# PV in groups of four heads, and a fifth late bank per block, with the quartic of three of the five on GpSimd

## Chip, cores and metric

One core of a Trainium2 chip. The metric is the device time of one execution, in us (median of the runs).

## The reference

One transformer block of 2048 tokens, width 448, on a layer-normalized input: attention with 16 heads of 28, and a gated two-layer GELU network of width 1792.

```python
xn = _layernorm(A_x)
scores = jnp.einsum("bhqd,bhkd->bhqk", q, k) * Dh ** -0.5     # 16 heads, 2048 x 2048
o = jnp.einsum("bhqk,bhkd->bhqd", _softmax(scores), v)
s = o.transpose(...).reshape(B, S, D) @ wo
g = _silu(_gelu(xn @ w1 + b1) @ w2 + b2)
return x + s * g
```

## The kernel before

The attention is 16 blocks (4 groups of 4 heads, by 4 chunks of 512 queries). A block has 64 banks: 16 key tiles of 128 keys for each of 4 heads, each bank 128 keys by 512 queries of scores in PSUM. Bank m belongs to head m % 4. The banks go round in a ring of six. They are handled in units of three (`UB`), two in block 0: TensorE writes a unit of scores, ScalarE turns it into P with one exponential, and TensorE multiplies P with V (PV) into one accumulator, with head j in column group 32 j.

Four banks of each of the blocks 1 to 14 are *late*: ScalarE leaves them out, and VectorE works out the exponential as a quartic polynomial, in six passes.

```python
# late bank: evacuation, then p_exp2 (all on VectorE)
tensor_scalar(ysb, ring, c0, c1, mult, add)                   # L991, frees the PSUM bank
tensor_scalar(v, ylo, EXP_SC / 65536.0, None, mult)           # L1004
scalar_tensor_tensor(u, v, EXP_A, v, add, mult)               # L1005
scalar_tensor_tensor(u, u, EXP_B, u, add, mult)               # L1007
scalar_tensor_tensor(u, v, EXP_D, u, mult, add)               # L1009
scalar_tensor_tensor(plate, ysb, 2.0 ** -9, u, mult, add)     # L1011, bf16 bits of the exponential
# then one PV matmul of its own for this bank, when it is ready (L1019)
...
# p_exps: ScalarE, one unit                                     L969
eng.activation(K.P[:, p0:p0 + n, :], K.ring[:, b0:b0 + n, :], ACTF.Exp, scale=SM_SCALE)
...
# p_pv: one group of PV matmuls for each unit, so 3 heads at a time, or 2 (L1052)
```

The order of each engine's program is fixed when the kernel is built. A list scheduler runs through all tasks with an assumed duration for each, and emits next the task that it believes can start first (among tasks of that engine within 0.1 us of it, the one of highest priority). On the chip each engine then works through its program in that order and waits on semaphores. So an assumed duration does not change what is computed, but it decides where in an engine's program a task stands.

## Time and profile before

| | before |
|---|---|
| time, us | 507.67 |
| profiled span, us | 505.4 |
| ScalarE busy, us | 478.8 |
| TensorE / VectorE / GpSimd busy, us | 452.5 / 379.0 / 74.2 |
| waits of ScalarE for scores, us | 7.4 |
| granted TensorE clock (share of full speed) | 0.965 |

ScalarE is busy for 95% of the span and hardly waits, so its work sets the time. TensorE also looks full, but it waits for ScalarE.

### The profile page before, as it was taken

The page shows a single profiled execution, that of the slowest core. Times are in us where ns is not written, and L with a number is a line of the kernel's source. Part 1 is how long each engine was busy: PE and PEld are TensorE (multiplying, and loading weights), DVE is VectorE, ACT ScalarE, POOL GpSimd, SP SyncE. Part 2 cuts the span into 40 slices and gives each one's busy share as a digit, 9 for nine tenths or more (in the row PEclk, how much of TensorE's full clock was granted, in tenths as well). Part 3 has the DMA queues.
Part 4 walks back from the last instruction along what each step waited for, and adds up shares of the span by engine and source line. Part 5 has one row for each costly group of instructions (what it writes and reads, how often), then busy time and mean ns, then how long its engine had stood idle before and what let it go on. Part 6 is the DMA issues. An engine that isn't in the chain of part 4 may idle for free.

```text
span 505.4 us, 8696 instructions
## 1 busy us (share of the span) xinstructions
PE 452.5 (90%) x3507; PEld 146.0 (29%) x3507; DVE 379.0 (75%) x640; ACT 478.8 (95%) x385; POOL 74.2 (15%) x93
## 2 busy tenths in 40 slices
PE   6899899998999999999999999766999999999884
PEld 2433223332222222222222222212333233332442
DVE  6823997879688898988888888832576868588545
ACT  3899999999999999999999999997899999999993
POOL 5661311031011111011101010211001001010100
PEclk9999999999699999999999999956999999999989
DMA  8801000000000000000000000000001010101211
GB/s 249 258 11 23 1 1 1 0 1 1 2 1 0 1 0 1 2 2 0 1 1 0 1 3 0 1 0 0 1 2 36 2 36 2 38 0 38 75 40 36
DMA packets 8503, 10.98 MB, mean 22 GB/s; under 512 B 2448, under 2 KB 6992, under 8 KB 8464
## 3 DMA queue, kind: packets, MB, share of 16 engines
q1 hardware_dynamic: 8464, 10.44, 6.8%
q8 instruction: 27, 0.44, 0.4%
q14 instruction: 12, 0.10, 0.1%
HBM read 8.61 MB, written 1.84 MB: 21 GB/s over the span
## 4 chain that ended last, share of the span: by engine, by line
PE 39%; ACT 38%; issue 15%; DVE 7%; ACTq 0%; DVEq 0%
ACT P L969 38%; PE ring L942 9%; PE misc L890 9%; PE acc L1052 7%; PE misc L627 3%; PE misc L847 3%; PE acc L714 1%; PE acc L1019 1%; DVE qT L793 1%; DVE qT L783 1%; PE ring L627 1%; DVE w L1087 1%; DVE x_sb L1009 1%; DVE x_sb L991 1%; PE ring L807 1%
## 5 line engine op out<-in xcount | busy, mean ns | idle before, releaser
L969 ACT ACTIVATE P<-ring 128x1536 bf16<-128x1536 f32 (+1 forms) x352 | 438.0, 1473 | 7.7 <-PE ring L942 7.4
L942 PE MATMUL ring<-qT,kT 32*128 32x512 bf16 (+1 forms) x1216 | 139.1, 355 | 25.6 <-ACT P L969 20.9
L1052 PE MATMUL acc<-P,vaug 128*32 128x512 bf16 (+1 forms) x1160 | 130.9, 355 | 0.0
L942 PEld LDWEIGHTS ring<-qT,kT 32*128 32x128 bf16 x1216 | 37.1, 92 | 148.4 <-ACT P L969 127.7
L847 PE MATMUL misc<-xnT,w 128*128 128x512 bf16 x224 | 63.5, 388 | 0.4 <-DVE qT L793 0.2
L890 PE MATMUL misc<-w,h 128*128 128x448 bf16 x224 | 54.6, 363 | 2.7 <-DVE qT L783 0.9
L1052 PEld LDWEIGHTS acc<-P,vaug 128*32 128x32 bf16 x1160 | 33.2, 94 | 64.7 <-issue 60.7
L991 DVE TENSOR_SCALAR x_sb<-ring 128x512 int32<-128x512 f32 x56 | 38.6, 689 | 17.4 <-PE ring L942 16.3
L860 DVE TENSOR_SCALAR h<-misc,b1c 128x512 bf16<-128x512 f32 x56 | 41.8, 747 | 11.8 <-PE misc L847 11.4
L1113 POOL CAST rhi<-rc 128x512 bf16<-128x512 f32 x15 | 13.4, 891 | 245.0 <-DVE rc L1109 169.8
L1005 DVE SCALAR_TENSOR_TENSOR x_sb<-x_sb 128x512 f32<-128x512 f32 x56 | 41.8, 746 | 1.0
L1011 DVE SCALAR_TENSOR_TENSOR x_sb<-x_sb 128x512 uint16<-128x512 int32 x56 | 41.1, 734 | 1.0
L1009 DVE SCALAR_TENSOR_TENSOR x_sb<-x_sb 128x512 f32<-128x512 f32 x56 | 40.9, 730 | 0.9
L1007 DVE SCALAR_TENSOR_TENSOR x_sb<-x_sb 128x512 f32<-128x512 f32 x56 | 40.7, 727 | 1.1
L788 POOL TENSOR_TENSOR qsq<-qT 128x512 bf16<-128x512 bf16 x15 | 18.6, 1243 | 141.8 <-DVE qT L783 110.6
L890 PEld LDWEIGHTS misc<-w,h 128*128 128x128 bf16 x224 | 17.2, 99 | 28.9 <-issue 14.7
L895 DVE TENSOR_TENSOR w<-misc,b2b 128x448 bf16<-128x448 f32 x16 | 10.0, 622 | 19.7 <-PE misc L890 19.5
L1004 DVE TENSOR_SCALAR x_sb<-x_sb 128x512 f32<-128x512 uint16 x56 | 24.4, 436 | 0.2
L872 ACT ACTIVATE h<-h 128x7168 bf16<-128x7168 bf16 x4 | 24.4, 6164 | 0.0
L847 PEld LDWEIGHTS misc<-xnT,w 128*128 128x128 bf16 x224 | 15.5, 98 | 29.4 <-issue 11.2
L1019 PE MATMUL acc<-x_sb,vaug 128*32 128x512 bf16 x56 | 21.9, 392 | 0.2 <-DVE x_sb L1011 0.2
L627 PE MATMUL misc<-xnT,wq 128*128 128x512 bf16 x56 | 17.6, 435 | 2.7 <-DVE qT L793 1.7
(127 smaller groups left out, 336.4 us busy)
## 6 DMA issues: line engine op xcount, KB each, us to landing
x_sb<-in_A_x_dram SPq DMA_DIRECT2D x4, 448.0 KB, 6.4
h<-in_A_x_dram SPq DMA_DIRECT2D x4, 448.0 KB, 3.3
w<-in_B_w_dram SPq DMA_DIRECT2D x1, 1568.0 KB, 12.8
w<-in_B_w_dram SPq DMA_DIRECT2D x1, 1344.0 KB, 7.3
out_dram<-h SPq DMA_DIRECT2D x6, 224.0 KB, 1.9
h<-in_A_wqkv_dram SPq DMA_DIRECT2D x1, 672.0 KB, 4.8
out_dram<-h SPq DMA_DIRECT2D x4, 112.0 KB, 1.7
wo<-in_A_wo_dram SPq DMA_DIRECT2D x16, 24.5 KB
```

The costliest lines, as they stand in the source:

```text
L627: ins = eng.matmul(bank, w[:, kt, g * 128:(g + 1) * 128], K.xnT[:, kt, c * 512:(c + 1) * 512], start=(kt == 0), stop=(kt == KT - 1))
L847: ins = eng.matmul(bank, K.w1[:, kt, ft * 128:(ft + 1) * 128], K.xnT[:, kt, c * 512:(c + 1) * 512], start=(kt == 0), stop=(kt == KT - 1))
L860: yield _Task(DVE, lambda eng: eng.tensor_scalar(dst, bank, K.b1c[:, ft:ft + 1], None, op0=ALU.add), [tok, K.b_b1c], wr, 0.75, 0.0, 2)
L890: ins = eng.matmul(ps, hv[:, ft, t * 128:(t + 1) * 128], K.w2[:, ft, :], start=(ft == 0), stop=(ft == FT - 1))
L942: return eng.matmul(K.ring[:, RB[m], col:col + nq], K.kT[32 * j:32 * j + 32, g, t * 128:(t + 1) * 128], K.qT[32 * j:32 * j + 32, g, c * 51 ...
L969: return eng.activation(K.P[:, p0:p0 + n, :], K.ring[:, b0:b0 + n, :], ACTF.Exp, scale=SM_SCALE)
L991: yield _Task(DVE, lambda eng, m=m, i=i: eng.tensor_scalar(K.ysb[i], K.ring[:, RB[m], :], SM_SCALE * LOG2E * 65536.0, 127.0 * 65536.0, op0 ...
L1005: yield _Task(DVE, lambda eng: eng.scalar_tensor_tensor(u, v, EXP_A, v, op0=ALU.add, op1=ALU.mult), [tv], [tu], 0.75, 0.0, 4)
L1007: yield _Task(DVE, lambda eng: eng.scalar_tensor_tensor(u, u, EXP_B, u, op0=ALU.add, op1=ALU.mult), [tu], [tu], 0.75, 0.0, 4)
L1009: yield _Task(DVE, lambda eng: eng.scalar_tensor_tensor(u, v, EXP_D, u, op0=ALU.mult, op1=ALU.add), [tv, tu], [tu], 0.75, 0.0, 4)
L1011: yield _Task(DVE, lambda eng: eng.scalar_tensor_tensor(K.plate[k].bitcast(dt.uint16), y, 2.0 ** -9, u, op0=ALU.mult, op1=ALU.add), [ty, t ...
L1052: return eng.matmul(K.acc[32 * j:32 * j + 32, q0:q0 + nq], K.vaug[:, t, 4 * g + j, :], K.P[:, PB[m], col:col + nq], tile_position=(0, 32 * ...
```

## The change

The intent is to take more exponentials from ScalarE. A fifth late bank per block is not expected to fit on VectorE, so in blocks 4 to 14 GpSimd takes the middle of three of the five; VectorE keeps their first and last pass. PV runs over four heads at a time, and a late bank fills the place in a group that another late bank of the same head has left free.

```diff
-    for _r in (5, 17, 29, 41): ...
-        LATE.add(_m)
+    if _b < C:
+        LATE.update(range(_m, 64 * _b + 46, 12))       # four, on VectorE
+    else:
+        LATE.update((_m + 6, _m + 30))                 # two on VectorE
+        GP.update((_m, _m + 18, _m + 36))              # three with GpSimd
...
+    def p_gexp2(self, m, i):
+        def ts(o, a, s0, s1, op0, op1, rd, wr):        # GpSimd, planned with 0.72 us
+        def tt(o, a, b, op, rd, wr):                   # GpSimd, planned with 1.1 us
+        yield ts(v, lo, EXP_SC / 65536.0, 0.5 * EXP_A, ALU.mult, ALU.add, [ty], [tv])
+        yield tt(z, v, v, ALU.mult, [tv], [tz])
+        yield ts(z, z, EXP_C, None, ALU.add, ALU.bypass, [tz], [tz])
+        yield tt(z, z, v, ALU.mult, [tv, tz], [tz])
+        yield ts(z, z, EXP_D, None, ALU.add, ALU.bypass, [tz], [tz])
+        yield tt(z, z, v, ALU.mult, [tv, tz], [tz])
+        yield ts(z, z, EXP_E, None, ALU.add, ALU.bypass, [tz], [tz])
+        # last pass on VectorE: plate = y * 2^-9 + z
...
-        for u in range(NU):                            # PV by units of three
+        for q in range(MTOT // 4):                     # PV by four heads, late banks in the holes,
+            ms = list(range(4 * q, 4 * q + 4))         # or as a fifth matmul of the group
```

The new buffers `v` and `z` (512 fp32 each) lie in the keys of group 0, which nothing reads from block 4 on.

More of the change, by code (lines that the diff above doesn't have):

```diff
@@ L29 @@
 MTOT = NBLK * T * 4
-LATE = set()
+LATE, GP = set(), set()
 for _b in range(1, NBLK - 1):
-    for _r in (5, 17, 29, 41):
-        _m = 64 * _b + _r
-        while (_m - 64) % UB != UB - 1:
-            _m += 1
-        LATE.add(_m)
-UNITS, RB, PB, RPREV, PPREV = [], {}, {}, {}, {}
+    _m = 64 * _b + 4
+    while (_m - 64) % UB != UB - 1:
+        _m += 1
+    if _b < C:
[3 more added lines that the diff above has]
+        GP.update((_m, _m + 18, _m + 36))
+LATE |= GP
+UNITS, RB, PB, RPREV, PPREV, UOF = [], {}, {}, {}, {}, {}
 _last, _plast, _p = {}, {}, 0
@@ L48 @@
     for _k, m in enumerate(_ms):
+        UOF[m] = len(UNITS) - 1
         RB[m] = _b0 + _k
@@ L60 @@
 EXP_SC, EXP_A, EXP_B, EXP_D = 1.1449707906804418, 2.2275165815584925, 18.59640770523752, -75.73931899211772
+EXP_C = EXP_B - 0.5 * EXP_A * EXP_A
+EXP_E = -0.25 * EXP_A * EXP_A * (EXP_B - 0.25 * EXP_A * EXP_A) - 0.5 * EXP_A * EXP_D
 LN_EPS = 1e-5
@@ L322, in alloc @@
         self.plate = [xf[:, 5120 + 512 * i:5632 + 512 * i] for i in range(4)]
+        self.pv_, self.pz = (self.kT[:, 0, 1024 * i:1024 * (i + 1)].bitcast(f32) for i in range(2))
         self.x2 = self.h[:, :, 3584:5376].rearrange("p c (t d) -> p c t d", d=D)
         self.b_y, self.b_pl = [B() for _ in range(3)], [B() for _ in range(4)]
-        self.b_ev, self.b_eu = B(), B()
+        self.b_ev, self.b_eu, self.b_pv, self.b_pz = B(), B(), B(), B()
         self.b_xn = [[B() for _ in range(4)] for _ in range(3)]
@@ L363, in schedule @@
         K.exp_u = -1
+        K.exp_m = -1
+        K.late_ready = []
+        K.gfree = True
         K.sc_u = -1
@@ L974, in p_exps @@
             K.exp_u = u
+            K.exp_m = UNITS[u][0][-1]
             if u >= NU - 2:
@@ L994, in p_late @@
                 K.ring_rel[m] = True
-                K.spawn(K.p_exp2(m, i), m)
+                K.spawn(K.p_gexp2(m, i) if m in GP else K.p_exp2(m, i), m)
+    def p_gexp2(self, m, i):
+        K = self
+        yield ("until", lambda: len(K.pls) > 0 and K.gfree)
+        K.gfree = False
+        k = K.pls.pop(0)
+        v, z, y, lo = K.pv_, K.pz, K.ysb[i], K.ylo[i]
+        tv, tz, ty = K.b_pv, K.b_pz, K.b_y[i]
+        if tv.w is None:
+            for c in range(C):
+                tv.r += K.b_kT[0][c].r
+                tz.r += K.b_kT[0][c].r
+        def ts(o, a, s0, s1, op0, op1, rd, wr):
+            return _Task(POOL, lambda eng: eng.tensor_scalar(o, a, s0, s1, op0=op0, op1=op1), rd, wr, 0.72, 0.0, 4)
+        def tt(o, a, b, op, rd, wr):
+            return _Task(POOL, lambda eng: eng.tensor_tensor(o, a, b, op), rd, wr, 1.1, 0.0, 4)
+        yield ts(v, lo, EXP_SC / 65536.0, 0.5 * EXP_A, ALU.mult, ALU.add, [ty], [tv])
[5 more added lines that the diff above has]
+        yield ts(z, z, EXP_E, None, ALU.add, ALU.bypass, [tz], [tz])
+        yield _Task(DVE, lambda eng: eng.scalar_tensor_tensor(K.plate[k].bitcast(dt.uint16), y, 2.0 ** -9, z,
+                                                              op0=ALU.mult, op1=ALU.add),
+                    [ty, tz], [K.b_pl[k]], 0.75, 0.0, 3)
+        K.ys.append(i)
+        K.gfree = True
+        K.late_ready.append((m, k))
     def p_exp2(self, m, i):
@@ L1015, in p_exp2 @@
         K.ys.append(i)
-        b, j, pc, end, s = K.pieces(m)
-        g, t = b // C, pc[0][0]
-        yield ("until", lambda: K.pv_done[64 * b + 3] and K.ready([K.b_pl[k]], 0.1))
-        yield _Task(PE, lambda eng: eng.matmul(K.acc[32 * j:32 * j + 32, :], K.vaug[:, t, 4 * g + j, :], K.plate[k],
-                                               tile_position=(0, 32 * j), start=False, stop=False, skip_group_check=True),
-                    [K.b_pl[k], K.b_v[0 if g == 0 else 1][t]], [K.b_acc], 0.25, 0.1, 1.2)
-        K.pls.append(k)
-        K.late_left[b] -= 1
+        K.late_ready.append((m, k))
     def p_pv(self):
@@ L1030, in p_pv @@
         K.pv_started = True
-        for u in range(NU):
-            ms = UNITS[u][1]
-            parts, cur = [], []
-            for m in ms:
-                cur.append(m)
-                if K.pieces(m)[3]:
-                    parts.append(cur)
-                    cur = []
-            parts.append(cur)
-            for part in parts:
-                if not part:
-                    continue
-                first = K.sub_of(part[0])
-                yield ("until", lambda: K.exp_u >= u and K.E_done >= first - 1 and (
-                    not K.pieces(part[-1])[3] or K.late_left[part[-1] // 64] == 0))
-                fl, rd = [], []
-                for m in part:
-                    b, j, pc, end, s = K.pieces(m)
-                    g = b // C
-                    for t, q0, nq, col in pc:
-                        def f(eng, m=m, t=t, j=j, g=g, q0=q0, nq=nq, col=col):
-                            return eng.matmul(K.acc[32 * j:32 * j + 32, q0:q0 + nq], K.vaug[:, t, 4 * g + j, :],
-                                              K.P[:, PB[m], col:col + nq],
-                                              tile_position=(0, 32 * j), start=(t == 0), stop=(t == T - 1),
-                                              skip_group_check=True)
-                        fl.append(f)
-                        rd += [K.b_P[PB[m]], K.b_v[0 if g == 0 else 1][t]]
-                def fall(eng, fl=fl):
-                    ins = None
-                    for f in fl:
-                        ins = f(eng)
-                    return ins
-                yield _Task(PE, fall, rd, [K.b_acc], 0.18 + 0.05 * len(part) + 0.02 * (len(fl) - len(part)), 0.1,
-                            lambda: 1.2 if K.exp_u - K.pv_u > 4 else 6)
-                for m in part:
-                    K.pv_done[m] = True
-                if end:
-                    K.spawn(K.p_epi(b) if b < NBLK - 1 else K.p_epi4(s), 0.5)
-            K.pv_u = u
@@ new lines, in p_pv, with f, fall @@
+        for q in range(MTOT // 4):
+            ms = list(range(4 * q, 4 * q + 4))
+            first, end = K.sub_of(ms[0]), K.pieces(ms[-1])[3]
+            b = q // 16
+            yield ("until", lambda: K.exp_m >= ms[-1] and K.E_done >= first - 1 and (
+                not end or len([x for x in K.late_ready if x[0] // 64 == b]) == K.late_left[b]))
+            late = []
+            for m, k in list(K.late_ready):
+                hole = (4 * q + m % 4) in LATE and all(m % 4 != x[0] % 4 for x in late)
+                if m // 64 == b and (end or len(K.late_ready) - len(late) > 2 or (
+                        hole and K.ready([K.b_pl[k]]))):
+                    late.append((m, k))
+            for x in late:
+                K.late_ready.remove(x)
+            K.late_left[b] -= len(late)
+            src = [(m, K.P[:, PB[m], :], K.b_P[PB[m]]) for m in ms if m not in LATE]
+            src += [(m, K.plate[k], K.b_pl[k]) for m, k in late]
+            src = sorted(src[:4], key=lambda x: x[0] % 4) + src[4:]
+            fl, rd = [], []
+            for kk in range(4):
+                for m, ap, tok in src:
+                    _, j, pc, _, s = K.pieces(m)
+                    g = b // C
+                    if kk >= len(pc):
+                        continue
+                    t, q0, nq, col = pc[kk]
+                    def f(eng, t=t, j=j, g=g, q0=q0, nq=nq, col=col, ap=ap):
+                        return eng.matmul(K.acc[32 * j:32 * j + 32, q0:q0 + nq], K.vaug[:, t, 4 * g + j, :],
+                                          ap[:, col:col + nq], tile_position=(0, 32 * j), start=(t == 0),
+                                          stop=(t == T - 1), skip_group_check=True)
+                    fl.append(f)
+                    rd += [tok, K.b_v[0 if g == 0 else 1][t]]
+            def fall(eng, fl=fl):
+                ins = None
+                for f in fl:
+                    ins = f(eng)
+                return ins
+            yield _Task(PE, fall, rd, [K.b_acc], 0.36 if len(fl) < 5 else 0.6, 0.1,
+                        lambda: 1.2 if K.exp_u - K.pv_u > 4 else 6)
+            for m in ms:
+                K.pv_done[m] = True
+            K.pls += [k for _, k in late]
+            K.pv_u = UOF[ms[-1]]
+            if end:
+                K.spawn(K.p_epi(b) if b < NBLK - 1 else K.p_epi4(first - NBLK + 1), 0.5)
```

## The prediction

> **What bounds the kernel now.** I read the page's busy shares first, then the groups split by shape, then who waited for whom, then the timeline of ScalarE, and last the timelines of GpSimd and VectorE. The busy line of the page:
>
> ```profile
> PE 452.5 (90%) x3507; PEld 146.0 (29%) x3507; DVE 379.0 (75%) x640; ACT 478.8 (95%) x385; POOL 74.2 (15%) x93
> ```
>
> Two engines look full, TensorE (90%) and ScalarE (95%). The groups and ScalarE's own waits tell which one sets the time:
>
> ```profile
> L969 ACT ACTIVATE P<-ring 128x1536 bf16<-128x1536 f32 x264 | 368.4, 1590 | 7.3 <-PE ring L942 7.0
> L969 ACT ACTIVATE P<-ring 128x1024 bf16<-128x1024 f32 x88 | 96.1, 1123 | 0.4 <-PE ring L942 0.3
> ...
> PEld ring L942 <- ACT P L969: 127.7, 282, 1.1
> ...
> ACT P L969 <- PE ring L942: 7.4, 7, 4.8
> ```
>
> 352 exponentials wait for TensorE 7 times, 7.4 us in all, 4.8 us of it once. TensorE's score matmuls wait 282 times for ScalarE to release a bank, 0.45 us each on average (127.7 / 282). So ScalarE is the bound and TensorE runs ahead of it. ScalarE's timeline shows the same in long unbroken stretches:
>
> ```profile
> 49.24 83.48 ACT L969 ACTIVATE P<-ring 128x1536 bf16<-128x1536 f32 x66 [0.49 <-PE ring L942]
> 133.82 187.40 ACT L969 ACTIVATE P<-ring 128x1536 bf16<-128x1536 f32 x148 [1.10 <-PE ring L942]
> 321.23 1.28 ACT L872 ACT_TABLE_LOAD   x1
> 322.53 24.38 ACT L872 ACTIVATE h<-h 128x7168 bf16<-128x7168 bf16 x4
> 346.92 1.28 ACT L874 ACT_TABLE_LOAD   x1
> 348.21 2.37 ACT L969 ACTIVATE P<-ring 128x1536 bf16<-128x1536 f32 x2
> 355.33 17.83 ACT L969 ACTIVATE P<-ring 128x1536 bf16<-128x1536 f32 x14 [4.75 <-PE ring L942]
> ```
>
> The records overlap, so their mean (1590 ns) is not the pitch. Starts seen one by one in the timeline give it: 199.31, 200.65, 201.98 (three-bank units, 1.33 us apart), 202.88 (0.90 us after a two-bank one). One bank is 1.33 - 0.90 = 0.43 us of ScalarE. The other holes are a start of some 15 us with few exponentials, the 1.1 us at 133 (granted clock 0.67 there), the 4.75 us after the GELU (clock 0.5 until about 350), and a tail of some 9 us after the last exponential.
>
> **What the Trainium skill says.** Three places bear on it.
> "SBUF — State Buffer", section "Who interferes with whom": a VectorE instruction with two SBUF inputs and a GpSimd instruction that reads SBUF exclude each other for a whole instruction; the one that comes second waits. The trace agrees:
>
> ```profile
> 203.10 1.15 POOL L788 TENSOR_TENSOR qsq<-qT 128x512 bf16<-128x512 bf16 x1 [10.16 <-DVE qT L783]
> ...
> 203.39 1.41 DVE L1005 SCALAR_TENSOR_TENSOR x_sb<-x_sb 128x512 f32<-128x512 f32 x1
> ```
>
> L1005 usually takes 0.69 us (median of its 56); begun 0.29 us after the GpSimd product it takes 1.41, that is it waits until about 204.1 and then runs its 0.69. A VectorE evacuation from PSUM beside the same kind of product kept its usual 0.74 us.
> "GPSIMD Engine Reference", section "Engine selection": two-input elementwise work is about twice as slow there as on VectorE, one-input work about as fast. In the trace the two-input forms take 1.04 us at best against 0.69 (1.5 times), and a one-input, two-operation tensor_scalar of 448 columns 0.718.
> "TensorE: Matmul & The Clock Gate", Part 3: small matmuls in different column groups run at the same time, so a fourth tile is nearly free. Here a PV group of three heads shows 0.40 us, five or six matmuls 0.61, eight 0.82: about 0.21 us for each pass, whatever it holds.
>
> **The change part by part.**
> *Late banks.* Before: four per block in blocks 1 to 14, 56. After: four in blocks 1 to 3 and five in 4 to 14, 12 + 55 = 67. ScalarE loses 11 banks: 11 x 0.43 = 4.7 us. Of a block of ScalarE time, 17.33 x 1.33 + 4 x 0.90 = 26.7 us, 26.3 remain. This is on the path and is the one gain I count in full.
> *VectorE.* A late bank now costs L991, L1004, L1005, L1007, L1009, L1011: 0.69 + 0.44 + 0.75 + 0.73 + 0.73 + 0.73 = 4.07 us, 56 times, 228 us. After, 34 of this kind (138 us) and 33 that keep only the first and last pass, 1.42 us each (47 us): 185 us, 43 less. VectorE is not the bound, so this buys slack only, and part of it goes back into waits for the shared port.
> *GpSimd.* 33 chains of four tensor_scalar and three products. Estimated tensor_scalar at 512 columns, from the 448-column row and the 0.23 us of the 1-column ones: 0.23 + 512 x (0.718 - 0.23) / 448 = 0.79. A product is 1.05 at its fastest, and each dependent step adds about 0.08 (the gap between the cast L1113 and the difference L1114). Chain: 4 x 0.79 + 3 x 1.05 + 7 x 0.08 = 6.9 us. Per block three chains, 20.6 us, and the work it has already, 0.61 + 1.05 for the normalization and about half a square of q, 2.3 us: 23 of 26.3 us without contention. VectorE's two-input passes after the change hold the shared port for about (2 x 3 + 5) x 0.69 = 7.6 us of a block, 29%. If a GpSimd step meets one with that chance and waits half of it, that is 0.1 us a step, 2.1 us a block. So 25 of 26.3 us: tight, but it should fit. A chain with its two VectorE passes is then some 7.6 + 1.4 = 9 us.
> *PV.* Passes before: about one for each of the 352 units and one for each of the 56 late banks, some 410. After: 256 groups of four heads, in whose holes most late banks fit, and perhaps 30 additional passes. 120 passes of 0.21 us, about 25 us of TensorE, all beside ScalarE work: it takes away some of the 90% and lets TensorE wait longer for banks. On the path only in the 7.4 us that ScalarE waits; I count nothing.
> *Cost of lateness.* The order of each engine's instructions is fixed beforehand with assumed durations: in the diff 0.72 for a GpSimd tensor_scalar and 1.1 for a product, so 6.2 us and some 0.5 for steps. The real chain is by my estimate 0.2 to 1 us longer, and queues add to it by the third chain of a block. The last pass on VectorE, the PV group that takes the bank and the normalization's matmuls stand in fixed places and would wait. TensorE has about 0.45 us of slack per unit, so only a lag beyond that reaches ScalarE. If one chain in ten costs 0.45 us that is 1.5 us for 33; with queues in the normalization counted too I put it at 1.5 us in all, a choice and not a measurement.
>
> Sum: 507.8 - 4.7 + 1.5 = 504.6, say **504.5 us**.
>
> **The rivals.**
> *GpSimd becomes the bound.* For: 25 of 26.3 us is already 95%, and the shared port is claimed by both engines; the records of L1114 have a median of 1.37 us against a minimum of 1.05, and the cast L1113 0.94 against 0.61, so waiting is usual even now. If every step waits as those do (0.33 us), a chain is 6.9 + 7 x 0.33 = 9.2 us and a block needs 27.6 + 2.3 = 30 us, 3.6 more than ScalarE: some 40 us in 11 blocks, 540 us. Against: these waits come while VectorE does 16 us of late passes per block; after the change it does 8 + 4. A middle case, 1 us per block over, gives 514.
> *The waits move into the fixed order.* GpSimd keeps up on average, but each late chain holds VectorE (last pass) or TensorE (PV, normalization) for 1 to 2 us. VectorE then evacuates projections late, TensorE waits for a bank and ScalarE for scores. With 0.3 us for each of 33 chains, 10 us: 513. Against: today's collisions of 0.7 us on VectorE leave ScalarE unbroken for 187 us.
> *The hole after the GELU closes.* TensorE, freed of PV passes, may have scores ready there: up to 4.75 us more gain, 500. Against: that hole comes from a long chain of projections and the 14 matmuls of one output tile at half clock, put before the scores; PV has no part in it. It can as well grow by a few us with the new order.
> *PV in four makes TensorE the gain.* If TensorE were the true bound, 25 us would come off, 480. The 282 waits of TensorE for ScalarE speak against it.
>
> **Range and chances.** The best case is 4.7 us and most of the GELU hole, about 500; the usual one 503 to 506; the two bad rivals 510 to 515, which I give one chance in six together. Range 500.5 to 511. Faster by over 2% needs under 497.7, which the 4.7 us cannot give even with the whole of the hole and nothing lost elsewhere: 3%. Slower by over 2% is over 518, GpSimd well over its block: 7%. Within: 90%.
>
> **What would show it right or wrong.** Right: 253 three-bank units where there were 264 and 99 of two banks, pitches still 1.33 and 0.90; ScalarE's waits for scores still below 10 us; GpSimd busy some 230 to 270 us more, in blocks 4 to 14, with chains of about 7 us and idle time at the end of each block; VectorE's busy time down by 30 to 40 us; fewer PV passes and TensorE waiting longer for ScalarE. Wrong: ScalarE's waits at some 15 us or more, with VectorE waiting for GpSimd before its last pass or TensorE for late banks; GpSimd without idle time between chains; GpSimd products well over 1.4 us.

## More of the kernel before

The experiments ran in three rounds, each on another chip and each with the kernel before beside them (e1 to e4: 507.86 us, e5 to e8: 508.11, e9 to e12: 508.14). In the round of the changed kernel the kernel before takes 507.67 us (four runs, 507.16 to 508.96).

## The result

The changed kernel takes 595.26 us (four runs, 594.31 to 597.43). The ratio is 1.173 (95% interval 1.169 to 1.177). Here and below, a ratio is the mean time of one kernel's fast runs over that of the other's of the same rounds, so it is not quite the ratio of the medians quoted. The result is correct.

The busy line of the page, after the change:

```profile
PE 463.8 (78%) x3507; PEld 147.2 (25%) x3507; DVE 371.9 (63%) x574; ACT 482.9 (82%) x385; POOL 386.0 (65%) x324
```

ScalarE fell from 95% to 82%, GpSimd rose from 15% to 65%. GpSimd's 65% is an average over a span in which the chains run only from 134 us on, and pause from 382 to 416 us, at the GELU (369 to 394) and after it. From the waits after the change (engine and line, what it waited for, us in all, times, longest):

```profile
ACT P L980 <- PE ring L953: 90.8, 61, 7.8
DVE x_sb L1033 <- POOL kT L1022: 77.8, 32, 4.3
...
PEld misc L858 <- DVE h L871: 30.2, 27, 3.8
```

This is a chain of waits. VectorE stands before its last pass (L1033) until GpSimd has finished, 32 times of 33 and 2.4 us each. Meanwhile it does not evacuate projections (L871), TensorE waits for their bank (30.2 us, 5.1 before), the scores behind them come late, and ScalarE waits 90.8 us where it had waited 7.4. The chain of work that ended last, of the page, names the source:

```profile
POOL 54%; PE 18%; ACT 11%; issue 9%; DVE 8%; POOLq 0%; ACTq 0%; DVEq 0%
POOL kT L1022 30%; POOL kT L1025 21%; ACT P L980 10%; PE misc L901 4%; PE ring L953 3%; PE acc L1095 3%; POOL rlo L1157 2%; DVE x_sb L1033 2%; PE misc L638 1%; POOL rhi L1156 1%; PE acc L725 1%; DVE x_sb L1003 1%; PE misc L858 1%; PE misc L1181 1%; DVE h L871 1%
```

GpSimd is not in that line of the profile of before (TensorE 39%, ScalarE 38%, issue 15%, VectorE 7%). One chain, from GpSimd's timeline (start, duration, line, operation):

```profile
157.37 0.94 POOL L1022 TENSOR_SCALAR kT<-x_sb 128x512 f32<-128x512 uint16 x1
158.40 1.35 POOL L1025 TENSOR_TENSOR kT<-kT 128x512 f32<-128x512 f32 x1
159.84 1.81 POOL L1022 TENSOR_SCALAR kT<-kT 128x512 f32<-128x512 f32 x1
161.73 1.26 POOL L1025 TENSOR_TENSOR kT<-kT 128x512 f32<-128x512 f32 x1
163.08 1.49 POOL L1022 TENSOR_SCALAR kT<-kT 128x512 f32<-128x512 f32 x1
164.65 1.26 POOL L1025 TENSOR_TENSOR kT<-kT 128x512 f32<-128x512 f32 x1
166.00 1.49 POOL L1022 TENSOR_SCALAR kT<-kT 128x512 f32<-128x512 f32 x1
```

It takes 10.1 us (157.37 to 167.49). The three additions of a constant take 1.49 to 1.81 us each. The first step, an operation of the same name with *two* arithmetic operations, took 0.62 us when nothing disturbed it. Chains start 11.7 us apart on average (134.21 to 227.88, eight intervals), with other GpSimd work between them. Three of them are 35 us, and a block of ScalarE has 26.3. That is 8.8 us too much in each of 11 blocks, 97 us as a rough estimate.

### The profile page after: what moved, and what is told of

The parts are those of the page before. It is cut to its first block, busy times and chain, and to the rows that moved or that the text cites. A ratio compares the mean times of both kernels' runs of the same rounds, so it can differ in the third digit from the quotient of the medians.

```text
span 592.5 us, 8929 instructions
## 1 busy us (share of the span) xinstructions
PE 463.8 (78%) x3507; PEld 147.2 (25%) x3507; DVE 371.9 (63%) x574; ACT 482.9 (82%) x385; POOL 386.0 (65%) x324
## 4 chain that ended last, share of the span: by engine, by line
POOL 54%; PE 18%; ACT 11%; issue 9%; DVE 8%; POOLq 0%; ACTq 0%; DVEq 0%
POOL kT L1022 30%; POOL kT L1025 21%; ACT P L980 10%; PE misc L901 4%; PE ring L953 3%; PE acc L1095 3%; POOL rlo L1157 2%; DVE x_sb L1033 2%; PE misc L638 1%; POOL rhi L1156 1%; PE acc L725 1%; DVE x_sb L1003 1%; PE misc L858 1%; PE misc L1181 1%; DVE h L871 1%
## 5 line engine op out<-in xcount | busy, mean ns | idle before, releaser
L980 ACT ACTIVATE P<-ring 128x1536 bf16<-128x1536 f32 (+1 forms) x352 | 441.5, 1364 | 92.4 <-PE ring L953 90.8
L953 PE MATMUL ring<-qT,kT 32*128 32x512 bf16 (+1 forms) x1216 | 150.6, 385 | 31.5 <-ACT P L980 25.3
L1022 POOL TENSOR_SCALAR kT<-kT 128x512 f32<-128x512 f32 x99 | 155.9, 1574 | 8.3
L1025 POOL TENSOR_TENSOR kT<-kT 128x512 f32<-128x512 f32 x99 | 130.3, 1316 | 7.7
L1095 PE MATMUL acc<-P,vaug 128*32 128x512 bf16 (+1 forms) x1149 | 107.4, 388 | 3.2 <-DVE x_sb L1033 2.5
L858 PE MATMUL misc<-xnT,w 128*128 128x512 bf16 x224 | 73.1, 443 | 28.7 <-DVE h L871 20.7
L1022 POOL TENSOR_SCALAR kT<-x_sb 128x512 f32<-128x512 uint16 x33 | 30.9, 938 | 66.9 <-DVE x_sb L1003 44.8
L1033 DVE SCALAR_TENSOR_TENSOR x_sb<-x_sb,kT 128x512 uint16<-128x512 int32 x33 | 25.2, 765 | 77.8 <-POOL kT L1022 77.8
L871 DVE TENSOR_SCALAR h<-misc,b1c 128x512 bf16<-128x512 f32 x56 | 41.8, 746 | 30.2 <-PE misc L858 30.1
L1003 DVE TENSOR_SCALAR x_sb<-ring 128x512 int32<-128x512 f32 x67 | 45.9, 685 | 22.1 <-PE ring L953 22.0
L858 PEld LDWEIGHTS misc<-xnT,w 128*128 128x128 bf16 x224 | 17.2, 104 | 64.0 <-DVE h L871 30.2
L1054 DVE SCALAR_TENSOR_TENSOR x_sb<-x_sb 128x512 uint16<-128x512 int32 x34 | 32.2, 948 | 0.6
L1050 DVE SCALAR_TENSOR_TENSOR x_sb<-x_sb 128x512 f32<-128x512 f32 x34 | 30.6, 899 | 0.5
L1052 DVE SCALAR_TENSOR_TENSOR x_sb<-x_sb 128x512 f32<-128x512 f32 x34 | 30.1, 886 | 0.4
L1048 DVE SCALAR_TENSOR_TENSOR x_sb<-x_sb 128x512 f32<-128x512 f32 x34 | 29.2, 859 | 0.4
```

Of the source, the lines that this page charges most:

```text
L858: ins = eng.matmul(bank, K.w1[:, kt, ft * 128:(ft + 1) * 128], K.xnT[:, kt, c * 512:(c + 1) * 512], start=(kt == 0), stop=(kt == KT - 1))
L871: yield _Task(DVE, lambda eng: eng.tensor_scalar(dst, bank, K.b1c[:, ft:ft + 1], None, op0=ALU.add), [tok, K.b_b1c], wr, 0.75, 0.0, 2)
L953: return eng.matmul(K.ring[:, RB[m], col:col + nq], K.kT[32 * j:32 * j + 32, g, t * 128:(t + 1) * 128], K.qT[32 * j:32 * j + 32, g, c * 51 ...
L980: return eng.activation(K.P[:, p0:p0 + n, :], K.ring[:, b0:b0 + n, :], ACTF.Exp, scale=SM_SCALE)
L1003: yield _Task(DVE, lambda eng, m=m, i=i: eng.tensor_scalar(K.ysb[i], K.ring[:, RB[m], :], SM_SCALE * LOG2E * 65536.0, 127.0 * 65536.0, op0 ...
L1022: return _Task(POOL, lambda eng: eng.tensor_scalar(o, a, s0, s1, op0=op0, op1=op1), rd, wr, 0.72, 0.0, 4)
```

## The experiments

Theories: **F**, the one-operation form of the addition (second operation bypass) is slow in itself. **T**, additions with fp32 in and out, in place, are slow, whatever the form. **B**, GpSimd's throughput is the bound. **O**, the fixed order was planned with durations that are too short, and engines stand waiting at fixed places. **P**, GpSimd and VectorE lock each other out of a shared port. **V**, the new PV order is the loss.

| run | edit | us | ratio to before, 95% |
|---|---|---|---|
| changed kernel | | 595.26 | 1.173 (1.169 to 1.177) |
| e1_twoop | additions as two operations | 527.93 | 1.040 (1.037 to 1.042) |
| e2_pv4_only | PV in four, late banks as before | 506.49 | 0.998 (0.996 to 1.001) |
| e3_five_dve | five late banks, all on VectorE | 535.84 | 1.056 (1.053 to 1.059) |
| e4_one_gp | one chain per block in place of three | 563.59 | 1.109 (1.106 to 1.112) |
| e5_dur | changed kernel, planned with measured durations | 563.80 | 1.109 (1.105 to 1.112) |
| e6_twoop_dur | e1, planned with measured durations | 521.95 | 1.027 (1.025 to 1.030) |
| e7_one_gp_dur | e4, planned with measured durations | 532.34 | 1.047 (1.044 to 1.050) |
| e8_six | six steps in place of seven | 515.23 | 1.017 (1.012 to 1.023) |
| e9_memset | e8 with memsets for GpSimd's steps | 501.75 | 0.989 (0.987 to 0.991) |
| e10_two_gp | two six-step chains, three on VectorE | 519.18 | 1.022 (1.020 to 1.024) |
| e11_six_dve | e8, VectorE's durations planned too | 513.48 | 1.010 (1.008 to 1.012) |
| e12_late_tail | e2 with five late banks in blocks 12 to 14 | 523.80 | 1.031 (1.030 to 1.033) |

The time of e8 is the median of its three fast runs (513.98, 515.23, 518.96; with the slow one it is 517.09). The mean of the three gives 1.015.

All were found correct. In e9 the chains' banks are wrong on purpose: the polynomial is missing, and the last pass has little more than y * 2^-9 left. The check doesn't see this error in 33 of 1024 banks.

### e1_twoop: the form of the addition

```diff
-        yield ts(z, z, EXP_C, None, ALU.add, ALU.bypass, [tz], [tz])
+        yield ts(z, z, 1.0, EXP_C, ALU.mult, ALU.add, [tz], [tz])     # and so for EXP_D, EXP_E
```

> The three one-operation GpSimd additions (add a constant, second operation bypass; 1.49 us and more each in the trace) are written as multiply by 1.0 and add, the two-operation form of the chain's first step, which took 0.62 us at best. Nothing else, so every engine's order is the same. If the form is what costs (theory F): the additions fall to about 0.65 us, a chain from about 10.5 to about 7.5 us, GpSimd no longer sets the time, and the whole takes 503 to 515 us with the granted clock back over 0.94. If it is that input and output are both fp32, or in place (theory T), or waiting for the port shared with VectorE (theory P): the additions stay at about 1.5 us and the time at 590 to 597 us.

Measured: 527.93 us, 67 us less than the changed kernel. GpSimd's groups split by shape, of the changed kernel and then of this one (line, operation, count, busy us and mean ns):

```profile
L1022 POOL TENSOR_SCALAR kT<-kT 128x512 f32<-128x512 f32 x99 | 155.9, 1574 | 8.3
L1025 POOL TENSOR_TENSOR kT<-kT 128x512 f32<-128x512 f32 x99 | 130.3, 1316 | 7.7
```

```profile
L1025 POOL TENSOR_TENSOR kT<-kT 128x512 f32<-128x512 f32 x99 | 131.4, 1328 | 10.1 <-DVE x_sb L1033 2.7
L1022 POOL TENSOR_SCALAR kT<-kT 128x512 f32<-128x512 f32 x99 | 73.9, 746 | 8.6
```

The addition fell from 1574 to 746 ns with the same buffers, type and place in the order; the products did not move. So F holds and T falls. The time stayed above the expected 503 to 515, so F is not all. Of the chain of work that ended last GpSimd still has 30%, after 54%.

### e2_pv4_only and e3_five_dve: without GpSimd

```diff
-    if _b < C:
-        LATE.update(range(_m, 64 * _b + 46, 12))
-    else: ...
+    LATE.update(range(_m, 64 * _b + 46, 12))                          # e2: four in every block
```
```diff
-                K.spawn(K.p_gexp2(m, i) if m in GP else K.p_exp2(m, i), m)
+                K.spawn(K.p_exp2(m, i), m)                            # e3: five, all on VectorE
```

> PV in groups of four with the four late banks per block of the kernel before in every block, all on VectorE, no GpSimd chain. If GpSimd's chains are the loss (F, T or P): 503 to 510 us, like the kernel before, with fewer PV passes on TensorE. If the new PV order, which waits for late banks inside a group, is the loss (theory V): 560 us or more.

> The changed kernel with all five late banks of blocks 4 to 14 on VectorE. VectorE then has 5 x 4.07 = 20.3 us of late passes in a block of 26.3 us plus some 6 us of other work, so it is just full: by F, T and P 503 to 525 us; by V 560 us or more. It tells what five late banks are worth without GpSimd.

e2 took 506.49 us and its interval includes 1: the new PV order costs nothing, and V falls. TensorE is busy 433.0 us where it was 452.5, and waits more for ScalarE; that gives nothing back, as it was not the bound.

e3 took 535.84, above the 503 to 525 expected. Its ScalarE waits:

```profile
ACT P L980 <- PE acc L1095: 22.8, 7, 5.9
...
ACT P L980 <- PE ring L953: 15.0, 17, 2.1
```

The first line is new: ScalarE waits for PV to free a buffer of P. In the new PV order the last PV group of a block is held until all five late banks are there. In its timeline the last pass of a late bank runs at 168.11, the PV groups with the late banks at 169.21 and 169.44, and the exponential that had waited 5.05 us at 170.39. From 135 to 315 us VectorE is busy 12.6 to 14.0 of each 15 us. In this order, then, VectorE alone doesn't deliver five late banks in time, which is the reason that the change has for using GpSimd; another order was not tried.

### e4_one_gp, e5_dur, e7_one_gp_dur: throughput or order

```diff
-        GP.update((_m, _m + 18, _m + 36))
+        GP.update((_m + 18,))                                         # e4 and e7
+        LATE.update((_m, _m + 36))
```
```diff
     def ts(...): ...
-        wr, 0.72, 0.0, 4)
+        wr, 0.94 if a is lo else 1.57, 0.0, 4)      # e5; in e7 0.78 and 1.63
     def tt(...): ...
-        wr, 1.1, 0.0, 4)
+        wr, 1.32, 0.0, 4)                           # e5; in e7 1.35
```

> One of the five late banks per block on GpSimd in place of three, four on VectorE. If GpSimd's throughput is the bound (F, T): one chain of some 10.5 us and 2.3 us of other work fit in a block of 26.3 us, so 503 to 515 us. If the loss goes by the number of chains that are late in a fixed order (theory O): a third of 87 us, some 535 us.

> The changed kernel, with the GpSimd durations that its fixed order is planned with set to the means of the trace after the change (first step 0.94 in place of 0.72, additions 1.57 for 0.72, products 1.32 for 1.1). The instructions are the same, only the order of each engine's program may change. If GpSimd's throughput is the bound (theory B: three chains of some 10.9 us do not fit in a block): 580 to 600 us, for the order cannot mend that. If it is the stale order (theory O: VectorE and TensorE stand waiting for late chains at fixed places): 540 us or less.

> One slow chain per block, four late banks on VectorE, planned with measured means (0.78, 1.63, 1.35). GpSimd was idle for two thirds of the time with the stale order, and the time was 563 us. By O the 31 us that VectorE waited for GpSimd vanish: 525 to 540 us (five banks on VectorE alone gave 536). By B or if it is contention at the shared port (P): 555 us or more.

e4 went against B: with one chain per block GpSimd is busy only 32% of the span, and yet the time is 563.59, more than with no chain at all (e3, 535.84). VectorE waited for every one of the eleven chains, 2.8 us each:

```profile
DVE x_sb L1034 <- POOL kT L1023: 31.2, 11, 4.3
```

With the durations mended (e7) 532.34 us are left, 31 us less, and of that wait 0.6 us are left: O in full for one chain.

e5 gives O a share in the changed kernel too: the same instructions, planned with measured durations, take 563.80 us, 31 us less. The rest, 56 us over the kernel before, stays: GpSimd is still busy 12.0 to 14.3 of each 15 us from 135 to 315 us, VectorE still waits 39.4 us for it, and ScalarE now waits in another place (36.0 us for PV to free P, 25.8 for scores). e5 alone doesn't show that this rest is B, for GpSimd has 26% of the chain that ended last, TensorE 27% and VectorE 21%. e6 below does: against e5 it differs in the form of the three additions, with durations planned to match, and takes 42 us less. So the theories are not exclusive: in the changed kernel about a third of the loss is the order, and about half is the length of GpSimd's steps, which this new order did not mend. My expectations put e5 at 540 or under for O or 580 and over for B; it fell between.

### e6_twoop_dur and e8_six: a shorter chain, planned right

```diff
-        yield ts(z, z, 1.0, EXP_C, ...); yield tt(z, z, v, ALU.mult, ...)     # e6 keeps these, with
-        yield ts(z, z, 1.0, EXP_D, ...); yield tt(z, z, v, ALU.mult, ...)     # 0.89, 0.75 and 1.33
-        yield ts(z, z, 1.0, EXP_E, ...)                                       # as durations; e8 too
+        yield ts(K.pa, z, 1.0, EXP_C, ALU.mult, ALU.add, ...)                 # e8: w*w + C, in a new buffer pa
+        yield tt(z, z, K.pa, ALU.mult, ...)
+        yield ts(v, v, EXP_D, EXP_E, ALU.mult, ALU.add, ...)                  # D*w + E
+        yield tt(z, z, v, ALU.add, ...)
```

> The two-operation additions, planned with their measured means (0.89, 0.75, 1.33). Three chains are 3 x 7.8 = 23.4 us plus 2.9 us of other GpSimd work: 26.3 us, just the block. By O: the 22 us that VectorE waited for the last step go, 503 to 512 us. By B: GpSimd is still at the edge and the time stays at 518 to 528 us.

> A quartic in six GpSimd steps with only two-operation forms: w, w*w, w*w+C, times w*w, D*w+E, their sum; planned with the means of the two-operation run. A chain is three tensor_scalar at 0.75 to 0.9 and three two-input at 1.3 with six gaps, 6.8 us; three are 20.4 us, and with 2.9 us of other work 23.3 of the 26.3 us of a block. By B and O both: 501 to 506 us, better than the kernel before. If contention at the shared port (P) rules, not under 510.

e6: 521.95 us, 6 less than e1. The wait of VectorE for the last step fell from 21.8 to 9.1 us, but the time did not come down to the 503 to 512 that O alone would give; it is in the 518 to 528 of B. e8, with the shorter chain: 515.23 us, 7 less. GpSimd has idle time (busy 10.6 to 13.8 of each 15 us from 135 to 315 us, with its waits for the port in it), and still the kernel is 7 us slower than the one before, where B and O both said 501 to 506 and P not under 510. Something else costs. The two-input passes of VectorE's own late banks are the suspects: they take 0.88 to 1.02 us, where before they took 0.73 to 0.75.

### e9_memset: as busy, but reading nothing

```diff
-    return _Task(POOL, lambda eng: eng.tensor_scalar(o, a, s0, s1, op0=op0, op1=op1), ...)
+    return _Task(POOL, lambda eng: eng.memset(o.bitcast(bf16)[:, 0:768], 0.0), ...)
-    return _Task(POOL, lambda eng: eng.tensor_tensor(o, a, b, op), ...)
+    # two memsets of 650 elements, the second into the buffer pa
```

> The six-step kernel with each GpSimd step replaced by a memset of about the same length (768 elements, or two of 650; from 1.60 us for the 1792-element memset of the kernel before, an estimate of 0.73 and 1.28 us), same order, same waits. The late banks of the chains come out wrong on purpose. The GpSimd engine is as busy but reads no SBUF. If the rest of the six-step kernel's loss is the port that GpSimd and VectorE share (theory P): VectorE's two-input passes go back from 0.88 to 1.02 us each to about 0.7, and the time falls from 517 to 501 to 506 us. If it is the chain's length and order (B, O): 513 us or more.

The steps of the GpSimd chain are as long as in e8: 0.74 us for each memset of 768, 0.67 + 0.66 for two of 650, in all 6.2 us; in e8 0.81 + 0.73 + 0.72 + 2 x 1.29 + 1.41 = 6.3. The planned durations, and so the order, are those of e8. VectorE's four two-input passes of the quartic and their last pass with GpSimd's result, in e8 and then in e9:

```profile
L1055 DVE SCALAR_TENSOR_TENSOR x_sb<-x_sb 128x512 uint16<-128x512 int32 x34 | 34.7, 1020 | 0.6
L1051 DVE SCALAR_TENSOR_TENSOR x_sb<-x_sb 128x512 f32<-128x512 f32 x34 | 33.4, 983 | 0.5
L1053 DVE SCALAR_TENSOR_TENSOR x_sb<-x_sb 128x512 f32<-128x512 f32 x34 | 30.6, 900 | 0.4
L1049 DVE SCALAR_TENSOR_TENSOR x_sb<-x_sb 128x512 f32<-128x512 f32 x34 | 30.1, 885 | 0.4
L1034 DVE SCALAR_TENSOR_TENSOR x_sb<-x_sb,kT 128x512 uint16<-128x512 int32 x33 | 24.1, 730 | 9.4 <-POOL kT L1027 9.2
```

```profile
L1056 DVE SCALAR_TENSOR_TENSOR x_sb<-x_sb 128x512 f32<-128x512 f32 x34 | 26.1, 768 | 0.5
L1060 DVE SCALAR_TENSOR_TENSOR x_sb<-x_sb 128x512 uint16<-128x512 int32 x34 | 25.2, 743 | 0.6
L1054 DVE SCALAR_TENSOR_TENSOR x_sb<-x_sb 128x512 f32<-128x512 f32 x34 | 24.2, 713 | 0.4
L1058 DVE SCALAR_TENSOR_TENSOR x_sb<-x_sb 128x512 f32<-128x512 f32 x34 | 24.2, 713 | 0.4
L1039 DVE SCALAR_TENSOR_TENSOR x_sb<-x_sb,kT 128x512 uint16<-128x512 int32 x33 | 23.3, 705 | 5.3 <-POOL pa L1031 5.3
```

ScalarE's waits for scores, in e8 and then in e9:

```profile
ACT P L981 <- PE ring L954: 16.7, 18, 5.5
```

```profile
ACT P L981 <- PE ring L954: 8.9, 8, 3.4
```

The passes are back at 0.71 to 0.77 us, VectorE's busy time falls from 377.7 to 340.2 us, and the time from 515.23 to 501.75, 13.5 us (the slowest run of e9 is 10 us under the fastest of e8). The trace of e8 shows the cause instruction by instruction: of the two-input passes of the late banks, last pass included, those begun while a GpSimd instruction ran took 1.14 us in the mean (83), the others 0.68 (86); in e9 it is 0.77 and 0.68. VectorE's evacuations of L872, whose large operand comes from PSUM, took 0.75 us in both cases. The one-input pass from SBUF (L1004 of the kernel before) is stretched too, from a median of 0.42 to 0.80 us in e8, and beside memsets, in e9, to 0.55. So P is shown. Its 13.5 us hold a little more than the stretched passes: from its first step to its last, with the waits and other GpSimd work between, a chain takes 7.9 us in e8 and 7.2 in e9.

e9 is also the only run in which the fifth late bank pays. Its 501.75 lies 4.7 us under e2's 506.49, the 11 x 0.43 us of ScalarE that the prediction counted (e9 and e2 were timed in different rounds and on different chips, but the kernel before had 508.14 and 507.86 us in them). It is no usable kernel, as its late banks are wrong.

### e10, e11, e12: is there a version that keeps some of it?

```diff
-    [tv], [tu], 0.75, 0.0, 4)
+    [tv], [tu], 0.95, 0.0, 4)               # e11 and e10: VectorE's two-input passes as stretched
...                                           # and its one-input pass with 0.62 in place of 0.7
```
```diff
-        LATE.update((_m + 6, _m + 30)); GP.update((_m, _m + 18, _m + 36))
+        LATE.update((_m, _m + 18, _m + 36)); GP.update((_m + 6, _m + 30))     # e10, six-step chains
```
```diff
-    if _b < C:
+    if _b < 3 * C:                          # e12: four until block 11, then five, all on VectorE
```

> Five late banks, two of them on GpSimd in six steps and three on VectorE, planned with VectorE's stretched durations too (0.95 for two-input passes). GpSimd works 2 x 6.8 + 2.9 = 16.5 of 26.3 us, VectorE 3 x 4.07 + 2 x 1.42 = 15.0 us where it had 16.3 before. By P with half the collisions: 503 to 510 us. By B or O, now that both have room: 503 us.

> The six-step kernel, three chains, planned with VectorE's two-input passes at the 0.95 us that the trace shows under contention in place of 0.75. If the rest of the loss is that the order is stale for VectorE (O): 505 to 510 us. If VectorE's time itself is short under contention (P): 514 us or more.

> PV in groups of four, four late banks in blocks 1 to 11 and five in blocks 12 to 14, all on VectorE. After the GELU VectorE has no projections to evacuate: 12.2 of a block's 26 us were its other work and idle time. Three banks less on ScalarE, 1.3 us: 504 to 506 us if VectorE has the room, 508 or more if it has not.

e11: 513.48 us, between the two expectations. That is 2 us under e8's fast runs, in another round and with overlapping ranges (511.23 to 514.45, 513.98 to 518.96): the better order takes back little or nothing of what contention costs. e10 and e12 missed (519.18 and 523.80), and their traces say where. ScalarE's timeline shows the last of the four tanh instructions of the gate, in the kernel before and in e12:

```profile
449.15 1.70 ACT L904 ACTIVATE w<-w 128x1792 bf16<-128x1792 bf16 x1
```

```profile
500.00 1.70 ACT L915 ACTIVATE w<-w 128x1792 bf16<-128x1792 bf16 x1 [2.67 <-DVE w L906]
```

In e12 it comes after the last exponential (ended at 497.3) and everything that depends on it after that, so the tail from there to the end is 24 us long instead of 9. ScalarE's waits for scores before that are only 9.6 us. So e12 says nothing on whether VectorE had room; the planner put the work of the other half of the block too late. e10 has a similar tail (last exponential ended at 500.2 of a span of 516.6, 16 us), and its GELU starts at 349.8, 27 us later than before. Why the planner chose so I have not followed, and whether a mended e12 would win its 1.3 us stays open.

No version found beats the kernel before beyond doubt. e2, PV in four without the rest, is equal to it.

## Why the prediction was wrong

- *ScalarE is the bound, and a bank is worth 0.43 us.* Right for the kernel before; the changed kernel has another bound. 253 three-bank and 99 two-bank units ran, and e9 against e2 gives 4.7 us.
- *PV in four saves TensorE some 25 us and nothing of the time.* Right in kind: e2 shows 19.5 us less busy and a time equal to before.
- *GpSimd: "Estimated tensor_scalar at 512 columns, from the 448-column row".* This is the step that failed. I took a two-operation bf16 row for all four tensor_scalar steps and got 0.79 us; the first step fits (0.62 undisturbed), but the three one-operation additions took 1.49 undisturbed, 1.57 in the mean. Also, the 1.05 that I took for a product is that of a buffer with itself (1.04) or of the difference L1114, of a bf16 buffer and a 16-column one (1.05); a product of two fp32 buffers of 512 columns, written over one of them, took 1.26 undisturbed. The chain undisturbed is 0.62 + 1.04 + 2 x 1.26 + 3 x 1.49 + 7 x 0.08 = 9.2 us in place of 6.9, and three with the other work pass the 26.3 us of a block where I had 23. The form, mended alone, takes away 67 of the 88 us (changed kernel to e1). GpSimd's busy time rose by 312 us where I had 230 to 270.
- *Lateness: 1.5 us.* Off by more than ten times. The stale order is worth 31 us with slow chains (changed kernel to e5, and again e4 to e7), 6 us with fast ones (e1 to e6). I had reckoned one chain in ten late and 0.45 us for it; the trace has 32 of 33, 2.4 us each, and with room on GpSimd (e4) still 11 of 11, 2.8 us each. A duration that is planned too short is so for every chain, and not for some.
- *Contention: 2.1 us a block on GpSimd, and VectorE "not the bound, so this buys slack only".* The size for GpSimd was near: tensor_scalar steps of 0.62 undisturbed have a mean of 0.72 to 0.81 in e8, where I had 0.1 us a step. The second half was wrong. VectorE's busy time was to fall by 30 to 40 us; it fell by 7 in the changed kernel, and by 39 in e9, without the contention. The contention costs some 13 us (e8 to e9) although VectorE is busy for 74% only. The waits say how: with it ScalarE waits 16.7 us for scores, without it 8.9, for VectorE frees the banks that TensorE writes to.
- *The rival "GpSimd becomes the bound"* was the nearest, and its 540 us came from waits at the port alone; that its chain of 9.2 us agrees with the undisturbed 9.2 is a coincidence. I argued against it with lighter VectorE work. That argument looked at the wrong term: the step's own length. The rival "The waits move into the fixed order" came true beside it: it told the chain of waits as it was then seen, but with 0.3 us for each chain, 10 us in all, where the order was worth 31.
- *The clock.* It fell to 0.863, while TensorE's busy share fell from 90% to 78%. A somewhat lower clock did not cost time in e2 and e9: they have 0.936 and 0.931, under the 0.965 of before, and are not slower. Why it fell, and whether 0.863 costs something, no run shows.

From the changed kernel to the gain it was meant to have: 595.3, two-operation form 527.9, mended order 522.0, one step less 515.2, no reading beside VectorE 501.8. The shares depend on this sequence: order alone, taken first, gives 31 us (e5).

## What to carry to other kernels

Take the cost of a moved operation from its own form (operations, types, one buffer or two) on its new engine; if the trace has no such row, measure it first, for a neighbouring form can be off by a factor of two. In a program of fixed order, wrong assumed durations of the new work cost time of their own (6 to 31 us here), so correct them from the first trace and build again. And work moved from VectorE to GpSimd was not parallel where both read SBUF (passes of 0.68 us took 1.14 beside GpSimd): count it on one port, and mind what waits for the engine that is stretched, even if its busy share is well under 100%.

## What the Trainium skill lacked or had wrong

- "GPSIMD Engine Reference", section "Elementwise — side-by-side cycle accounting": it gives a body of up to two operations 1.03 cycles per element. For 512 columns at the page's 1.2 GHz that is 0.44 us, an estimate without start-up. The two-operation tensor_scalar is near it (0.62 us for 512 columns undisturbed), but one operation with bypass took 1.49 us undisturbed (mean 1.57; 0.746 in two-operation form in the same place). The page has nothing on this form; "Engine selection" calls one-input work roughly line-rate without that exception.
- The same section gives one cost for two-input work, about 2.6 cycles per element. In these traces, 512 columns each and undisturbed, a buffer times itself took 1.04 us and two different fp32 buffers 1.26 us. The second writes over one of its inputs and the first does not; which of the two differences counts was not tried.
- "SBUF — State Buffer", section "Who interferes with whom", was right: two-input VectorE passes have means of 0.71 to 0.77 us beside memsets and of 0.88 to 1.02 us beside GpSimd steps that read. It does not say that this can cost some 13 of 515 us while neither engine is full (VectorE 74%, GpSimd 55%).
